# A causal softmax convolution and a gated two-matrix product on one core: an earlier pace for block 5's input, paired tiles in the narrow round, one evicting engine per pair in block 0, and another order of the first copies

## Chip, core and metric

The kernel runs on one core of a Trainium2 chip. The metric is the device time of one execution in microseconds (us), as the median of several executions; lower is better. A profile is taken from one separate execution, so its times belong to that execution.

## What is computed

The input `x` is 8 sequences of 3904 rows and 192 columns. Each group of 24 columns (a head, 8 of them) has 7 taps; the taps pass through a softmax, and every output row is the weighted sum of the row and the six before it. The result, flattened to 31232 rows, goes through a gated product and two more matrices.

```
w   = softmax(weight, axis=-1)                      # 8 heads x 7 taps
c[b, s, h, :] = sum_k w[h, k] * x_pad[b, s + k, h, :]   # six zero rows before each sequence
a, b = c @ w1, c @ w2                               # 192 -> 1024
h    = (a * b) @ w3                                 # 1024 -> 1024
out  = h @ w_out                                    # 1024 -> 192
```

Inputs and output are fp32; the kernel multiplies in bf16 and accumulates in fp32.

## The kernel before

The kernel is one program whose instruction order on every engine is written out by hand. `w3 @ w_out` is folded into one 1024x192 matrix `W_sb` once (`w3_product`, from a transposed `w3T`), so that the main work per row is one product with `w1`, one with `w2`, an elementwise product, and one with `W_sb`.

**Rows.** The 31232 rows are cut into two streams of 15616 rows (`NS = 2`), which lie in the two halves of the partitions. A round `R` is 512 columns (rows of the input) of both streams; there are 31 rounds, the last of them, round 30, has 256 columns. Rounds go in groups of four.

**Convolution.** It works on windows of 64 rows of which 58 are new, in blocks of windows (`SIZES`: 6, 4, 8, 10, 8, then six of 36, then 20). `load_x(b)` fetches a block's windows with DMAs from the POOL queue into `xb` tiles (five buffers). `conv` multiplies them with band matrices `Aband`, made from the taps by `band`, into PSUM, and ScalarE (ACT) or VectorE (DVE) copies the result to `convo`. In blocks 0 to 4 TensorE transposes `convo` into `xT` (`pe_transpose`, `joint_transposes`). From block 5 on, `store` writes `convo` to a DRAM tensor `rows` and `transposes` reads it back transposed by DMA from SP's queue.

**PSUM.** It is used as four pairs of banks (`banks()` takes a pair, `drained` gives it back). `move_all(p, moves, fs)` copies the parts of one pair with the engines named in `fs`, in order; `V`, `A` and `P` are copies on DVE, ACT and GpSimd (POOL).

**First product.** `first_part` makes one tile of 128 of the 1024 columns: for each of `w1` and `w2` six matmuls, three slices of 64 input columns (`k`) times two streams, 12 in all; ACT copies the first factor to `asb` (L390), DVE multiplies it with the second factor from PSUM into `abT` (L391). `first_rest` does the same for several tiles side by side in one pair of banks; before, only the rest of round 0 uses it. **Second product:** `second_product` multiplies `abT` by `W_sb` (L445), ACT evicts it (L450), a DMA writes it out.

**Prologue.** Block 0 is convolved, evicted, transposed and multiplied as early as its data arrive. `w1` and `w2` come in four parts of 256 columns. The first is cast from an fp32 tile; the other three are fetched by POOL's queue into partitions 0 to 63 (`load_w`) and copied to partitions 64 to 127 by POOL (`copy_w`, L193). The order on POOL is the order of these lines (L195 to L202):

```
    load_w(1)
    cast_w(1, 1, nc.gpsimd.tensor_copy)
    load_w(2)
    load_x(2, between=[seq((copy_w, 1, i, nc.gpsimd.tensor_copy) for i in range(2))])
    load_w(3)
    ...
```

`between` places the two copies of part 1 between the two DMAs of block 2. After that POOL issues `load_x(3)`, the two halves of `w3` to the DRAM tensor `w3rows` (L470), `load_x(4)` and more. SP's queue holds 16 DMA transposes of `w3rows` into `w3T` (L474): eight 128-column tiles of the first half of its rows, then eight of the second half. Each half of them waits for its half of `w3rows`.

**Pace.** At L568 POOL copies two elements of `w3T` to a tiny tile `pace` just ahead of `load_x(5)` and `load_x(6)`, so that these ten DMAs start only when a certain transpose of `w3T` has landed:

```
    P(out=pace, in_=w3T[0:1, JT - 3, DFF - 2:DFF])
    load_x(5)
    load_x(6)
    first_product(3)
    ...
    zero(5)
    for jt in range(JT):
        w3_product(jt)
```

`JT` is 8, and the columns read belong to the second half, so this is the fourteenth transpose. `zero(5)` clears six rows in one of block 5's tiles, once per stream, behind all of `load_x(5)` and `load_x(6)` on POOL (L575). `w3_product(jt)` for `jt` below 4 reads transposes 1 to 8 and from `jt = 4` on transposes 9 to 16. The second products of rounds 0 to 3 follow, with the convolution of block 5 between them, three heads at a time.

**End.** The last group is rounds 28 to 30; its first products run in the order 30, 28, 29, and its second products close the program.

Of the kernel before, what the change touches and what calls it, by code (L numbers as in the profile page):

```python
# [16 lines left out]
def kernel(  # L17
# [10 lines left out]
    nc = tc.nc  # L28
# [42 lines left out]
    def banks():  # L71
        p = free.pop(0)
        return p, pairs[:, NS * p:NS * p + NS, :]
# [4 lines left out]
    def drained(p):  # L78
        assert p not in free
        free.append(p)  # L80
# [7 lines left out]
    def seq(fs):  # L88
        def run():
            for f, *a in fs:  # L90
                f(*a)
        return run
# [12 lines left out]
    def load_x(b, parts=(0, 1), between=()):  # L105
        between = list(between)
        tiles = xb_of.setdefault(b, [])
        zeros_of = zero_rows.setdefault(b, [])
        for i0, n in [v for e, v in enumerate(halves_of(b)) if e in parts]:
            xb = work.tile([128, n, D], BF16, tag="xb", bufs=5, name="xb")  # L110
            w = 0
            while w < n:
                i = i0 + w
                m = min(n - w, WB - i % WB)
                at_end = i + m == NWIN
                if at_end:
                    m -= 1
                if m:
                    for r in range(NS):
                        nc.gpsimd.dma_start(out=xb[Q * r:Q * r + Q, w:w + m, :],  # L120
                                            in_=x_spans(r, i, m))
                        if between:
                            between.pop(0)()
                if i % WB == 0:
                    zeros_of += [(xb, 0, w), (xb, 1, w)]
                w += m
                if at_end:
                    nc.gpsimd.memset(xb[Q:128, w, :], 0.0)
                    t = tok(NWIN - 1) - PAD
                    nc.gpsimd.dma_start(out=xb[0:Q, w, :], in_=x_rows[t:t + Q, :])  # L130
                    nc.gpsimd.dma_start(out=xb[Q:Q + PAD + LAST, w, :],
                                        in_=x_rows[TS + t:TS + t + PAD + LAST, :])
                    w += 1
            if len(halves_of(b)) == 1:
                tiles += [(xb, 0), (xb, SIZES[b] // 2)]
            else:
                tiles.append((xb, 0))
# [233 lines left out]
    def width(R):  # L371
        return min(CH, TS - R * CH)

    def first_part(R, ft, c0, c1, ks=tuple(range(NP))):
        ab = abT_of[R]
        r0 = (R * CH) % RING
        pq = []
        for i in range(2):
            q, p = banks()
            pq.append((q, p))  # L380
            for k in ks:
                for r in range(NS):
                    rs = slice(Q * r, Q * r + Q)
                    nc.tensor.matmul(  # L384
                        p[:, r, c0:c1], wd[i][rs, k, ft * 128:(ft + 1) * 128],
                        xT[k][rs, r0 + c0:r0 + c1],
                        start=(k == ks[0]), stop=(k == ks[-1]))
        (qa, pa), (qb, pb) = pq
        asb = work.tile([128, NS, CH], BF16, tag="asb", bufs=3, name="asb")
        nc.scalar.copy(out=asb[:, :, c0:c1], in_=pa[:, :, c0:c1])  # L390
        nc.vector.tensor_tensor(out=ab[:, ft, :, c0:c1], in0=asb[:, :, c0:c1],  # L391
                                in1=pb[:, :, c0:c1], op=ALU.mult)
        drained(qa)
        drained(qb)

    def first_rest(R, fts, c0, c1):
        ab = abT_of[R]
        r0 = (R * CH) % RING
        n, ne = c1 - c0, len(fts)
        assert ne * n <= CH  # L400
        pq = []
        for i in range(2):
            q, p = banks()
            pq.append((q, p))
            for e, ft in enumerate(fts):
                for k in range(NP):
                    for r in range(NS):
                        rs = slice(Q * r, Q * r + Q)
                        nc.tensor.matmul(  # L409
                            p[:, r, e * n:e * n + n], wd[i][rs, k, ft * 128:(ft + 1) * 128],  # L410
                            xT[k][rs, r0 + c0:r0 + c1], start=(k == 0), stop=(k == NP - 1))
        (qa, pa), (qb, pb) = pq
        asb = work.tile([128, NS, CH], BF16, tag="asb", bufs=3, name="asb")
        nc.scalar.copy(out=asb[:, :, 0:ne * n], in_=pa[:, :, 0:ne * n])
        a, b = (t[:, :, 0:ne * n].rearrange("p r (e c) -> p r e c", e=ne) for t in (asb, pb))
        nc.vector.tensor_tensor(
            out=ab[:, fts[0]:fts[0] + ne, :, c0:c1].rearrange("p e r c -> p r e c"),
            in0=a, in1=b, op=ALU.mult)
        drained(qa)
        drained(qb)  # L420

    def first_tile(R):
        abT_of[R] = work.tile([128, JT, NS, CH], BF16, tag="abT", bufs=GROUP, name="abT")
# [80 lines left out]
    def move_all(p, moves, fs):  # L504
        for f, m in zip(fs, moves):
            move(f, m)
        drained(p)

    def joint_transposes(b):
        n = SIZES[b] // 2  # L510
        assert n * NP <= 2 * CH // 64
        convo = convo_of[b]
        p, tps = banks()
        tps = bf16(tps)
        t0, moves = tok(FIRST[b]), []
        for k in range(NP):
            for w in range(n):
                nc.tensor.transpose(
                    out=tps[:, k * n + w, :],
                    in_=convo[:, w, k].rearrange("p r g -> p (r g)"), identity=ident)  # L520
            src = tps[:, k * n:k * n + n, :].rearrange("p w (c s) -> p c w s", c=2)
# [12 lines left out]
    first_part(0, 0, 0, EARLY, (0, 2, 1))  # L534
    move_all(*joint_transposes(1), (A, A, V))
    first_part(0, 1, 0, EARLY)
    first_rest(0, range(2), EARLY, CH)
    load_w3(0)
    for i in range(2):
        copy_w(3, i, P)  # L540
# [27 lines left out]
    P(out=pace, in_=w3T[0:1, JT - 3, DFF - 2:DFF])  # L568
    load_x(5)
    load_x(6)  # L570
    first_product(3)
# [70 lines left out]
```

## Time and profile before

| what | value |
|---|---|
| median of three runs | 523.0 us (522.9 to 523.83) |
| the profiled execution, its own time | 523.71 us |
| its span (first to last instruction) | 522.0 us |
| TensorE busy | 514.2 us, 98% of the span |
| VectorE busy | 358.1 us |
| ScalarE busy | 326.1 us |
| GpSimd busy | 58.6 us |
| granted TensorE clock | 0.998 |

The span leaves 1.7 us of the execution's own time outside. PE is TensorE and PEld its weight loads, DVE VectorE, ACT ScalarE, POOL GpSimd, SP SyncE; a name with a q (SPq, POOLq) is that engine's queue of DMA issues. L489 is line 489 of the kernel before. In the chain of waits each row is a start, a duration and what ran; in the timeline a row is start, duration, engine, line, operation, output and input, the count, and in brackets how long the engine had been idle and what ended that.

### The profile page before, as it was taken

To read this page: it belongs to the slowest core of one execution; us is meant where nothing else is said; L and a number is where in the kernel's file an instruction comes from. 1 tells how busy PE (TensorE), PEld (TensorE's weight loads), DVE (VectorE), ACT (ScalarE), POOL (GpSimd) and SP (SyncE) were. 2 spreads that over 40 slices of the span, in tenths; PEclk is the share of its full clock that TensorE was granted. 3 is DMA by queue.
4 is the path that set the end of the run, shared out by engine and by line. 5 is a ranking of instruction groups with operands and counts; after the bars stand their busy time and mean duration, and the time that the engine had idled before them with its cause. 6 is when DMAs were issued, how large, how long until landed. Compare 5 with 4: busy or idle time off the path is not lost.

```text
span 522.0 us, 13021 instructions
## 1 busy us (share of the span) xinstructions
PE 514.2 (98%) x5576; PEld 340.5 (65%) x5576; DVE 358.1 (69%) x347; ACT 326.1 (62%) x414; POOL 58.6 (11%) x98
## 2 busy tenths in 40 slices
PE   7999999999999999999999999999999999999997
PEld 4555788444894558845588455884558845599567
DVE  6778646799538995389953899438993299912870
ACT  6887642777437774377743777337774377735762
POOL 8601622030000200003000020001200000000000
PEclk9999999999999999999999999999999999999999
DMA  8979998699556973569645698456824532034004
GB/s 115 157 145 125 148 225 219 161 209 147 129 156 164 111 99 102 152 165 124 86 110 148 158 126 84 118 146 156 102 45 122 153 96 31 17 104 140 1 3 151
DMA packets 133420, 64.61 MB, mean 124 GB/s; under 512 B 90304, under 2 KB 132642, under 8 KB 133298
## 3 DMA queue, kind: packets, MB, share of 16 engines
q1 hardware_dynamic: 94320, 44.06, 35.0%
q0 software_dynamic: 38896, 19.62, 28.8%
q8 instruction: 43, 0.70, 0.6%
q14 instruction: 15, 0.12, 0.1%
q10 hardware_dynamic: 146, 0.10, 0.1%
HBM read 33.25 MB, written 36.52 MB: 134 GB/s over the span
## 4 chain that ended last, share of the span: by engine, by line
PE 90%; issue 3%; DMA 2%; DVE 2%; ACT 1%; POOL 1%; ACTq 0%; POOLq 0%; DVEq 0%
PE pairs L384 56%; PE pairs L445 31%; PE pairs L291 3%; DMA xb<-in_x_dram 2%; DVE abT L391 1%; ACT asb L390 1%; PE pairs L207 1%; POOL xb L120 0%; DVE cprod L248 0%; PE pairs L344 0%; ACT convo L312 0%; DVE convo L489 0%; POOL rows L335 0%; POOL wo_b L567 0%; PE pairs L409 0%
## 5 line engine op out<-in xcount | busy, mean ns | idle before, releaser
L391 DVE TENSOR_TENSOR abT<-asb,pairs 128x1024 bf16<-128x1024 bf16 (+2 forms) x248 | 297.9, 1201 | 76.8 <-ACT asb L390 39.9
L384 PE MATMUL pairs<-xT,wd 64*128 64x512 bf16 (+2 forms) x2976 | 319.4, 372 | 0.8 <-DVE abT L391 0.3
L390 ACT CAST asb<-pairs 128x1024 bf16<-128x1024 f32 (+2 forms) x248 | 247.1, 996 | 67.4 <-PE pairs L384 66.7
L384 PEld LDWEIGHTS <-wd 64*128 64x128 bf16 x2976 | 162.2, 94 | 151.4 <-issue 2.3
L445 PE MATMUL pairs<-W_sb,abT 128*128 128x192 bf16 x1952 | 166.1, 246 | 0.0
L445 PEld LDWEIGHTS <-abT 128*128 128x128 bf16 x1952 | 159.6, 98 | 9.7 <-issue 9.7
L450 ACT COPY osb<-pairs 128x384 f32<-128x384 f32 x122 | 58.3, 478 | 116.0 <-PE pairs L445 116.0
L312 DVE CAST convo<-pairs 128x864 bf16<-128x864 f32 (+5 forms) x67 | 50.8, 815 | 68.5 <-PE pairs L291 64.3
L120 POOL DMA_DIRECT2D xb<-in_x_dram x42 | 32.2, 782 | 6.4 <-PE pairs L384 3.7
L597 POOL COPY pace<-abT 1x2 bf16<-1x2 bf16 x10 | 1.8, 176 | 239.6 <-DVE abT L391 239.6
L291 PE MATMUL pairs<-xb,Aband 64*64 64x432 bf16 (+5 forms) x384 | 17.7, 284 | 0.5 <-POOL xb L575 0.5
L291 PEld LDWEIGHTS <-Aband 64*64 64x64 bf16 x384 | 7.2, 106 | 7.8 <-issue 6.6
L312 ACT CAST convo<-pairs 128x512 bf16<-128x512 f32 (+4 forms) x15 | 8.1, 584 | 1.3 <-PE pairs L291 1.2
L457 POOL DMA_DIRECT2D out_dram<-osb x8 | 6.1, 759 | 18.4 <-ACT osb L450 18.0
L450 DVE COPY osb<-pairs 128x192 f32<-128x192 f32 x1 | 0.4, 357 | 11.1 <-PE pairs L445 11.1
L480 PEld LDWEIGHTS <-w3T 128*128 128x128 bf16 x64 | 5.2, 98 | 0.4 <-issue 0.4
L480 PE MATMUL pairs<-wo_b,w3T 128*128 128x192 bf16 x64 | 5.5, 246 | 0.0
L344 PE MATMUL pairs<-ident,convo 128*128 128x128 bf16 x48 | 3.9, 219 | 1.4 <-DVE convo L489 1.3
L344 PEld LDWEIGHTS <-convo 128*128 128x128 bf16 x48 | 2.9, 97 | 3.2 <-DVE convo L489 1.6
L193 POOL COPY wd<-wd 64x768 bf16<-64x768 bf16 x6 | 4.8, 840 | 0.9 <-DMA wd<-in_moe_w_dram 0.9
L207 PE MATMUL pairs<-zeros 128*128 128x512 bf16 x8 | 3.8, 628 | 1.1 <-DVE ones L155 1.1
L482 ACT CAST W_sb<-pairs 128x192 bf16<-128x192 f32 x8 | 2.6, 319 | 2.8 <-PE pairs L480 2.8
(56 smaller groups left out, 42.0 us busy)
## 6 DMA issues: line engine op xcount, KB each, us to landing
out_dram<-osb SPq DMA_DIRECT2D x52, 384.0 KB
xb<-in_x_dram POOLq DMA_DIRECT2D x18, 432.0 KB, 7.5
rows<-convo SPq DMA_DIRECT2D x8, 648.0 KB
out_dram<-osb POOLq DMA_DIRECT2D x8, 384.0 KB, 4.8
w3rows<-in_moe_w_dram POOLq DMA_DIRECT2D x2, 1024.0 KB, 11.7
xb<-in_x_dram POOLq DMA_DIRECT2D x6, 240.0 KB, 5.3
rows<-convo SPq DMA_DIRECT2D x4, 324.0 KB
xT<-rows SPq DMA_TRANSPOSE x81
```

Source lines behind the costliest of these rows:

```text
L120: nc.gpsimd.dma_start(out=xb[Q * r:Q * r + Q, w:w + m, :], in_=x_spans(r, i, m))
L207: nc.tensor.matmul(t[:, j % 2, :], zeros, zeros[:, 0:1].to_broadcast([128, CH]), start=True, stop=True)
L291: nc.tensor.matmul(view(slice(Q * c, Q * c + Q), r)[:, :, j * G:(j + 1) * G], band_of(h, r), xb[Q * r:Q * r + Q, w0:w0 + n, h * G:(h + 1) ...
L312: f[e % len(f)](out=dst, in_=part)
L344: nc.tensor.transpose(out=tps[:, w, :], in_=convo[:, w, k].rearrange("p r g -> p (r g)"), identity=ident)
L384: nc.tensor.matmul(p[:, r, c0:c1], wd[i][rs, k, ft * 128:(ft + 1) * 128], xT[k][rs, r0 + c0:r0 + c1], start=(k == ks[0]), stop=(k == ks[-1]))
L390: nc.scalar.copy(out=asb[:, :, c0:c1], in_=pa[:, :, c0:c1])
L391: nc.vector.tensor_tensor(out=ab[:, ft, :, c0:c1], in0=asb[:, :, c0:c1], in1=pb[:, :, c0:c1], op=ALU.mult)
L445: nc.tensor.matmul(ops[:, (g - g0) * D:(g - g0) * D + D], ab[:, jt, r, g * 128:(g + 1) * 128], W_sb[:, jt, :], start=(jt == 0), stop=(jt = ...
L450: f(out=osb[:, g0:g0 + per, :].rearrange("p g d -> p (g d)"), in_=ops[:, 0:per * D])
L457: queue.dma_start(out=out[t0:t0 + ng * 128, :].rearrange("(g p) d -> p g d", p=128), in_=osb)
L480: nc.tensor.matmul(wps[:, 0, 0:D], w3T[:, gt, jt * 128:(jt + 1) * 128], wo_b[:, gt, :], start=(gt == 0), stop=(gt == JT - 1))
```

## The change

Five edits.

- POOL issues both DMAs of block 2 and then makes the two copies of part 1 (`between` goes away).
- In block 0, the pair of the first four heads is evicted by DVE alone and the pair of the last four by ACT alone; before, each pair was shared by both. The three transposed tiles are evicted in the order 0, 1, 2 by DVE, DVE, ACT, and the first tile of the product takes its slices in that order.
- `joint_transposes` (block 1) puts the third slice, which DVE evicts, into the pair's second bank.
- `first_part` and `first_rest` become one function over a list of tiles. `first_product` takes `512 // width` tiles at a time, so round 30 makes four pairs of 128-column tiles in place of eight single ones; other rounds are as before.
- `pace` reads the fourth transpose of the second half, the twelfth, in place of the fourteenth.

```diff
-    load_x(2, between=[seq((copy_w, 1, i, nc.gpsimd.tensor_copy) for i in range(2))])
+    load_x(2)
+    for i in range(2):
+        copy_w(1, i, nc.gpsimd.tensor_copy)
     load_w(3)
...
-    def first_part(R, ft, c0, c1, ks=tuple(range(NP))):
...
+    def first_factor(R, i, fts, c0, c1):
+        n, r0 = c1 - c0, (R * CH) % RING
+        assert len(fts) * n <= CH
+        q, p = banks()
+        for e, ft in enumerate(fts):
+            for k in range(NP):
                 for r in range(NS):
                     rs = slice(Q * r, Q * r + Q)
                     nc.tensor.matmul(
-                        p[:, r, c0:c1], wd[i][rs, k, ft * 128:(ft + 1) * 128],
-                        xT[k][rs, r0 + c0:r0 + c1],
-                        start=(k == ks[0]), stop=(k == ks[-1]))
+                        p[:, r, e * n:e * n + n], wd[i][rs, k, ft * 128:(ft + 1) * 128],
+                        xT[k][rs, r0 + c0:r0 + c1], start=(k == 0), stop=(k == NP - 1))
+        return q, p[:, :, 0:len(fts) * n]
...
+    def first_part(R, fts, c0, c1):
+        a, b = (first_factor(R, i, fts, c0, c1) for i in range(2))
+        first_times(R, fts, c0, c1, first_cast(*a), *b)
...
-        for ft in fts:
-            first_part(R, ft, 0, width(R))
+        N = width(R)
+        step = CH // N
+        for ft in fts[::step]:
+            first_part(R, list(range(ft, ft + step)), 0, N)
...
+        B2 = CH // 64
+        at = [0, n, B2]
...
-                    out=tps[:, k * n + w, :],
+                    out=tps[:, at[k] + w, :],
...
-    move_all(*conv(0, 0, 4, ()), (V, A))
-    move_all(*conv(0, 4, 4, ()), (A, V))
-    for k, f in ((0, A), (2, V), (1, V)):
+    move_all(*conv(0, 0, 4, ()), (V, V))
+    move_all(*conv(0, 4, 4, ()), (A, A))
+    for k, f in enumerate((V, V, A)):
         p, *m = pe_transpose(0, k)
...
-    first_part(0, 0, 0, EARLY, (0, 2, 1))
+    first_part(0, [0], 0, EARLY)
...
-    P(out=pace, in_=w3T[0:1, JT - 3, DFF - 2:DFF])
+    P(out=pace, in_=w3T[0:1, JT // 2 - 1, DFF - 2:DFF])
```

`first_cast` is ACT's copy to `asb` and `first_times` DVE's product, as they were inside `first_part` and `first_rest`.

More of the change, by code (lines that the diff above doesn't have):

```diff
@@ L103, in x_spans, with load_x @@
                        ap=[[D, Q], [ST * D, m], [1, D]])
-    def load_x(b, parts=(0, 1), between=()):
-        between = list(between)
+    def load_x(b, parts=(0, 1)):
         tiles = xb_of.setdefault(b, [])
@@ L121, in load_x @@
                                             in_=x_spans(r, i, m))
-                        if between:
-                            between.pop(0)()
                 if i % WB == 0:
@@ L372, in width @@
         return min(CH, TS - R * CH)
-    def first_part(R, ft, c0, c1, ks=tuple(range(NP))):
[L375 to L381, printed above, removed]
+    def first_factor(R, i, fts, c0, c1):
[4 more added lines that the diff above has]
+            for k in range(NP):
                 for r in range(NS):
@@ L384, in first_part, with first_cast @@
                     nc.tensor.matmul(
[L385 to L388 removed]
+                        p[:, r, e * n:e * n + n], wd[i][rs, k, ft * 128:(ft + 1) * 128],
+                        xT[k][rs, r0 + c0:r0 + c1], start=(k == 0), stop=(k == NP - 1))
+        return q, p[:, :, 0:len(fts) * n]
+    def first_cast(qa, pa):
@@ L389, in first_part @@
         asb = work.tile([128, NS, CH], BF16, tag="asb", bufs=3, name="asb")
-        nc.scalar.copy(out=asb[:, :, c0:c1], in_=pa[:, :, c0:c1])
-        nc.vector.tensor_tensor(out=ab[:, ft, :, c0:c1], in0=asb[:, :, c0:c1],
-                                in1=pb[:, :, c0:c1], op=ALU.mult)
+        asb = asb[:, :, 0:pa.shape[2]]
+        nc.scalar.copy(out=asb, in_=pa)
         drained(qa)
-        drained(qb)
[L396 to L420, printed above, removed]
@@ new lines, in first_cast, with first_times @@
+        return asb
+    def first_times(R, fts, c0, c1, asb, qb, pb):
+        ab, ne = abT_of[R], len(fts)
+        if ne == 1:
+            dst = ab[:, fts[0], :, c0:c1]
+        else:
+            dst = ab[:, fts[0]:fts[0] + ne, :, c0:c1].rearrange("p e r c -> p r e c")
+            asb, pb = (t.rearrange("p r (e c) -> p r e c", e=ne) for t in (asb, pb))
+        nc.vector.tensor_tensor(out=dst, in0=asb, in1=pb, op=ALU.mult)
+        drained(qb)
+    def first_part(R, fts, c0, c1):
+        a, b = (first_factor(R, i, fts, c0, c1) for i in range(2))
+        first_times(R, fts, c0, c1, first_cast(*a), *b)
@@ L510, in joint_transposes @@
         n = SIZES[b] // 2
-        assert n * NP <= 2 * CH // 64
+        B2 = CH // 64
+        at = [0, n, B2]
+        assert 2 * n <= B2
         convo = convo_of[b]
@@ L518, in joint_transposes @@
                 nc.tensor.transpose(
-                    out=tps[:, k * n + w, :],
+                    out=tps[:, at[k] + w, :],
                     in_=convo[:, w, k].rearrange("p r g -> p (r g)"), identity=ident)
-            src = tps[:, k * n:k * n + n, :].rearrange("p w (c s) -> p c w s", c=2)
+            src = tps[:, at[k]:at[k] + n, :].rearrange("p w (c s) -> p c w s", c=2)
             moves.append((xT[k][:, t0:t0 + 2 * n * ST].rearrange("p (c w s) -> p c w s", c=2, w=n),
@@ L533 @@
     first_tile(0)
-    first_part(0, 0, 0, EARLY, (0, 2, 1))
+    first_part(0, [0], 0, EARLY)
     move_all(*joint_transposes(1), (A, A, V))
-    first_part(0, 1, 0, EARLY)
-    first_rest(0, range(2), EARLY, CH)
+    first_part(0, [1], 0, EARLY)
+    first_part(0, [0, 1], EARLY, CH)
     load_w3(0)
```

## Prediction

> **What bounds the kernel now.** I read the page first, then the chain of waits, then the timeline where the chain leaves TensorE, last the DMA queues in windows. The page gives the frame.
>
> ```profile
> span 522.0 us, 13021 instructions
> PE 514.2 (98%) x5576; PEld 340.5 (65%) x5576; DVE 358.1 (69%) x347; ACT 326.1 (62%) x414; POOL 58.6 (11%) x98
> ```
>
> TensorE is busy for nearly all of the span, so an edit gains only where TensorE waits and nothing else holds the next step. The chain of waits (start, duration, what ran) shows those places.
>
> ```profile
> 7.43 0.57 DVE convo L489
> ...
> 8.03 0.55 ACT convo L489 x2
> ...
> 8.60 0.57 DVE convo L489
> ...
> 9.21 0.51 PE pairs L344 x6
> 9.72 0.37 PE pairs L291 x32
> 10.09 0.99 PE pairs L384 x12
> ...
> 13.46 1.96 PE pairs L384 x18
> ...
> 57.62 10.35 DMA xb<-in_x_dram
> ...
> 91.64 41.55 PE pairs L384 x384
> ...
> 478.41 1.11 PE pairs L384 x18
> 479.52 0.68 DVE abT L391
> ...
> 505.04 13.32 PE pairs L445 x160
> ```
>
> Three places: copies of block 0 one after another (7.43 to 9.17), the DMA of block 5's input (57.62 to 67.97), and DVE in the narrow round (478.41 to 505.04). Between the second and the third the chain is TensorE without a hole, so time won before 68 us stays won if block 5's input comes as much earlier.
>
> **Block 0's copies and the copy order.** The timeline of this stretch:
>
> ```profile
> 6.21 1.69 ACT L189 CAST wd<-wfirst 64x768 bf16<-64x768 f32 x2
> 8.45 0.47 ACT L489 COPY xT<-pairs 128x348 bf16<-128x348 bf16 x1
> 8.60 0.56 DVE L489 CAST convo<-pairs 128x384 bf16<-128x384 f32 x1 [0.61 <-ACT convo L489]
> 10.14 0.48 ACT L489 CAST convo<-pairs 128x384 bf16<-128x384 f32 x1 [1.22 <-PE pairs L291]
> 10.68 0.74 ACT L390 CAST asb<-pairs 128x696 bf16<-128x696 f32 x1
> 10.77 1.59 POOL L193 COPY wd<-wd 64x768 bf16<-64x768 bf16 x2 [0.86 <-DMA wd<-in_moe_w_dram]
> 11.45 0.88 DVE L391 TENSOR_TENSOR abT<-asb,pairs 128x696 bf16<-128x696 bf16 x1 [0.71 <-ACT asb L390]
> 12.31 0.68 POOL L120 DMA_DIRECT2D xb<-in_x_dram  x1
> ```
>
> Within a pair the engines take turns: ACT starts at 8.03 when DVE's copy of the first pair ends at 8.00, and DVE starts on the second pair at 8.60 when ACT ends at 8.57. With one engine per pair the two pairs go side by side. DVE ends its large copy at 8.00 as before; its small one (192 elements) costs between half of 0.57 and all of it; I take 0.3, so 8.3. ACT is free at 6.21 + 1.69 = 7.90; its small copy takes 0.55 / 2 = 0.27, the large one 0.48 (the row at 10.14, same shape), so it ends at about 8.67. The last transposes start at 8.7, not 9.21. Three of them (some 0.3) and block 1's convolution (0.37) end at 9.4. ACT evicts the last transposed slice in 0.47, by 9.5; the first product has then done two slices and ends its other 8 of 12 matmuls (0.66) at about 10.3, where it ended at 11.08 before: 0.8 earlier. ACT, though, has block 1's copy (0.48) behind that slice and starts `asb` at about 10.05, not 10.68: 0.63 earlier, and DVE and the next tiles hang on that. I take **0.6**, with 0.3 below (DVE's wait of 0.61 less ACT's small copy of 0.27) and 0.8 above.
>
> The bank for block 1's third slice I count at nothing: DVE copies it behind its own product, 11.45 to 12.33, so ACT has not been what it waits for. The three slices' order is in the sum above. POOL: the second DMA of block 2 (0.68 to issue) moves into the 0.86 that POOL idles before the copies, so the copies stay at 10.77 to 12.36 and everything issued behind them on POOL, the next part of the weights, block 3 and `w3`, goes out about 0.6 earlier. Tile 2, the first to need those copies, starts at 13.46 - 0.6 = 12.86; its cover is 0.5. As `w3` is fetched 0.6 earlier, its transposes start 0.6 earlier too; were that lost, the next part would come out smaller by it.
>
> **The pace.** The stretch around block 5, SP's queue, POOL and PE:
>
> ```profile
> 48.48 1.26 SPq L474 DMA_TRANSPOSE w3T<-w3rows  x1
> ...
> 51.09 1.26 SPq L474 DMA_TRANSPOSE w3T<-w3rows  x1
> ...
> 53.70 1.26 SPq L474 DMA_TRANSPOSE w3T<-w3rows  x1
> 53.86 0.18 POOL L568 COPY pace<-w3T 1x2 bf16<-1x2 bf16 x1 [12.02 <-DMA w3T<-w3rows]
> 54.39 6.21 POOL L120 DMA_DIRECT2D xb<-in_x_dram  x8 [0.36 <-issue]
> 59.56 5.45 PE L480 MATMUL pairs<-wo_b,w3T 128*128 128x192 bf16 x64
> 67.58 0.37 PE L291 MATMUL pairs<-xb,Aband 64*64 64x432 bf16 x2
> 68.52 0.25 POOL L575 MEMSET xb<- 6x192 bf16 x1 [0.26 <-DMA xb<-in_x_dram]
> 68.83 0.70 PE L291 MATMUL pairs<-xb,Aband 64*64 64x432 bf16 x9 [0.17 <-POOL xb L575]
> 72.20 0.74 PE L291 MATMUL pairs<-xb,Aband 64*64 64x432 bf16 x12
> ```
>
> Block 5's first 12 matmuls begin at 67.58 and end at 69.53, 1.95 where the next 12 (72.20) take 0.74: TensorE waits **1.21** for the input and the memset behind it. The twelfth transpose is issued 51.09 - 48.48 = 2.61 before the fourteenth, so `pace` and the first DMA come 2.61 earlier, on top of the 0.6. But at that time transposes still run, and they share the 16 DMA engines:
>
> ```profile
> q1 hardware_dynamic: 8704, 2.10, 45.4%
> ...
> q1 hardware_dynamic: 1094, 0.26, 31.7%
> ...
> q0 software_dynamic: 1486, 0.56, 157.9%
> ...
> q0 software_dynamic: 764, 0.29, 97.6%
> q1 hardware_dynamic: 501, 0.13, 41.6%
> ...
> q0 software_dynamic: 1220, 0.46, 156.6%
> q1 hardware_dynamic: 33, 0.00, 1.8%
> ```
>
> These are packets, MB and share of the engines' time in windows: the transposes from 27 to 57 us; of these, 53.3 to 57; then input DMAs (q0) alone, 173 to 176; input beside a transpose, 182.5 to 185; and input from 107.5 to 110 with a transpose issued. Input packets lag their issue by about 1.6 (issue at 54.39, first packets near 56), so in the present frame they would start at 53.3, with 1094 of 8704 packets, two of the 16 transposes, still to go. Alone, input moves 1486 / 3 = 495 packets per us; beside 501 transpose packets it moved 764 in 2.5 us where 1238 were due: 0.95 lost per transpose packet, so 1094 cost 1094 x 0.95 / 495 = 2.1. While the input's stream ramps up the loss is smaller; I take **1.85**, with 1.0 below and 2.6 (the whole lead) above. The input then lands 0.6 + 2.61 - 1.85 = 1.36 earlier. TensorE arrives 0.6 earlier and had 1.21 to wait, so at most 1.81 can be gained here; 1.36 is below that, and 0.45 of the wait remains. **Gain up to 69.5 us: 1.36**, from 0.3 (loss 2.6, transposes 0.3 earlier) to 1.8.
>
> The Trainium skill speaks against expecting more: DMA: Bandwidth & Descriptors, section "Queues, rings and completion order", has each DMA engine take turns between its queues packet by packet. By that rule each transpose packet would cost one input packet, 2.2 in all, and the gain here would be 1.0. The trace agrees at 182.5 (764 to 501) and not at 107.5 (1220 to 33).
>
> The last transpose: it feeds `w3_product` from the fifth column tile on, at 59.56 + 5.45 x 4.9 / 8 = 62.9, or 62.3 with the 0.6. Issued at 53.70, it lands by the lag of the fourteenth (51.09 to 53.86) near 56.4, or 55.8 with the 0.6. It would be late only if delayed by over 6; sharing as at 182.5 delays it by some 3, the 2.5 us of blocking at 107.5 on top gives 5.5. So the cover is thin, and I count nothing but keep it as the slower rival. Nothing else waits for POOL's earlier `pace`.
>
> **The narrow round.** From 478.41 to 505.04 are 26.63. At the pace of a full group, 41.55 / 384 = 0.1082 per matmul of 512 columns, its 192 full and 96 half-width matmuls take 20.78 + 5.19 = 25.97. DVE is the brake: 0.68 per half tile against 12 x 0.0541 = 0.65 on TensorE. In pairs round 30 has the instructions of half a full round, where no wait shows. I take **0.66**. Nothing is the lower end: 12 matmuls of 348 columns took 0.99 where the rate gives 0.88, and half-width ones may have such an excess of 12%. Loss is excluded: no engine gets more to do.
>
> **Sum.** 1.36 + 0.66 = 2.02. The profiled execution's span goes from 522.0 to 520.0, its own time from 523.71 to 521.7. It lies 0.7 above the median of 523.0; I put the same 2.0 off the median: **521.0**. With each term's ends: 0.3 + 0 to 1.8 + 0.66, thus 520.5 to 522.7.
>
> **Rivals.** (1) *The last transposes are blocked for as long as input is queued.* Blocks 5 and 6 are 36 windows each, 64 rows x 2 streams x 36 x 192 columns x 2 bytes = 1.77 MB, and at 0.56 MB in 3 us both take 19 us, from 52.7 to 71.7. TensorE would stand in `w3_product` from 62.3 to about 72.5, 10 late; it no longer waits for input, and 0.66 is won at the end: 10.2 - 1.8 - 0.66, about 7.7 slower, 530.7. For it speaks 107.5 to 110 with 33 packets to 1220; against it, at 182.5 the transpose went through with most of the input still ahead. It decides once the last transpose lands after 62.3; a delay of 9 takes the whole gain away. (2) *The early start only trades places*: the DMA engines do the same work before block 5 is in, the loss is the full 2.6 or over, and only 0.0 to 0.6 is won there: 521.7 to 522.5, say 522.0. For it: the loss by rule is already 2.2. Against: the transposes alone use the engines for a third to a half. (3) *The early copies reach nothing*, because some input of blocks 1 to 4 is late and the input of block 5 with it: 1.0 less, 522.1.
>
> **Chances.** Forecast 0.62, rival 1 0.18, rival 2 0.16, rival 3 0.04. About 0.2%, or 1.05 us, is what a measurement of this kernel can tell. The forecast lies over that; of rivals 2 and 3 I give 0.06 to faster and 0.14 to no change: faster 0.68, same 0.14, slower 0.18. The range: 520.3 at the low end, 0.2 beyond the full gain for the spread between executions, to 522.9, which takes in rivals 2 and 3 and the smallest gain; rival 1 is left out.
>
> **What would show it.** In the changed profile `asb` of the first tile starts near 10.05; `pace` ends its wait near 50.7; transposes 15 and 16 show issue times above 1.26; block 5's first 12 matmuls take about 1.2 and end near 68.2; round 30 shows no DVE on the chain and 25.97 up to the last second products. Wrong would be a hole in `w3_product` between its fourth and fifth tile (rival 1), or block 5's end at 69 or later (rival 2).

## The result and the profile after

The changed kernel takes **521.65 us** (median of 6 executions, 521.1 to 522.14); the kernel before took 523.5 on the same occasion (6 executions, 522.9 to 524.05). The ratio is 0.9965, 95% interval 0.9952 to 0.9978: 1.8 us faster. The profiled execution took 522.07 and had this page:

```profile
span 520.4 us, 13006 instructions
PE 513.5 (99%) x5576; PEld 339.8 (65%) x5576; DVE 357.5 (69%) x343; ACT 325.7 (63%) x410; POOL 58.4 (11%) x98
```

The span is 1.6 shorter, and the matmuls are the same 5576: what went is waiting. The chain of waits of the changed kernel (start, duration, what ran) says where. Its lines are numbered anew: L290 is the convolution, L381 the first product, L467 `w3_product`, L432 the second product.

```profile
5.19 4.20 DMA xb<-in_x_dram
...
9.43 0.44 PE pairs L290 x31
9.87 0.99 PE pairs L381 x12
...
59.41 5.39 PE pairs L467 x64
...
67.75 0.70 PE pairs L290 x9
...
90.57 41.55 PE pairs L381 x384
...
477.34 26.07 PE pairs L381 x288
503.41 13.32 PE pairs L432 x160
```

Block 0's copies, block 5's input and DVE in round 30 have left the chain. In front stands a new row, block 1's input, which lands at 9.39. The round's 288 matmuls take 26.07 where they took 26.63 from 478.41 to 505.04: **0.56**. The row 90.57 stood at 91.64: **1.07** came before it. Together 1.63, the span's 1.6.

The timeline of the prologue after (L476 is a copy out of PSUM, L389 makes `asb`, L457 issues a half of `w3`):

```profile
7.52 0.82 DVE L476 CAST convo<-pairs 128x384 bf16<-128x384 f32 x2 [0.25 <-PE pairs L290]
7.79 0.68 ACT L476 CAST convo<-pairs 128x192 bf16<-128x192 f32 x2
9.43 0.44 PE L290 MATMUL pairs<-xb,Aband 64*64 64x48 bf16 x31 [0.31 <-DMA xb<-in_x_dram]
10.46 0.74 ACT L389 CAST asb<-pairs 128x696 bf16<-128x696 f32 x1
16.29 0.55 POOL L457 DMA_DIRECT2D w3rows<-in_moe_w_dram  x1
```

The two pairs of block 0 are now evicted side by side, and both are out at 8.47 where the second ended at 9.16. In this execution TensorE then stands 0.31 for block 1's input, and `asb` starts only 0.22 earlier than before (10.68). The timeline around block 5 (L461 is a transpose of `w3`, L557 the `pace` copy, L564 the memset of `zero(5)`):

```profile
46.34 2.45 SPq L461 DMA_TRANSPOSE w3T<-w3rows  x1
51.22 0.17 POOL L557 COPY pace<-w3T 1x2 bf16<-1x2 bf16 x1 [9.60 <-DMA w3T<-w3rows]
51.75 7.17 POOL L119 DMA_DIRECT2D xb<-in_x_dram  x9 [0.36 <-PE pairs L381]
52.74 1.26 SPq L461 DMA_TRANSPOSE w3T<-w3rows  x1
59.34 5.45 PE L467 MATMUL pairs<-wo_b,w3T 128*128 128x192 bf16 x64
67.37 1.09 PE L290 MATMUL pairs<-xb,Aband 64*64 64x432 bf16 x12
67.45 0.25 POOL L564 MEMSET xb<- 6x192 bf16 x1 [0.34 <-DMA xb<-in_x_dram]
```

The twelfth transpose is issued at 46.34 and `pace` is released at 51.22, 4.88 later; the last is issued at 52.74 (53.70 in the kernel before). `w3_product` runs through in 5.45. Block 5's first 12 matmuls end at 68.46 instead of 69.53, and 1.09 - 0.74 = 0.35 of waiting is left. What the DMA queues moved meanwhile (packets, MB, share of the engines' time; q0 is the input, q1 the transposes), in the windows 54 to 55, 55 to 56, 56 to 57 and 58 to 59 us:

```profile
q0 software_dynamic: 248, 0.10, 87.0%
q1 hardware_dynamic: 12, 0.00, 1.6%
...
q0 software_dynamic: 476, 0.18, 156.2%
q1 hardware_dynamic: 19, 0.00, 2.6%
...
q0 software_dynamic: 500, 0.19, 156.8%
q1 hardware_dynamic: 6, 0.00, 1.1%
...
q0 software_dynamic: 277, 0.11, 85.5%
q1 hardware_dynamic: 271, 0.07, 53.4%
```

For 3 us what is left of the transposes, about the last one, hardly moves; in the last of these windows both queues get about as many packets. The Trainium skill, DMA: Bandwidth & Descriptors, section "Queues, rings and completion order", has an engine take turns between its queues packet by packet. If the profile's packets are the ones meant there, which no run here shows, 277 to 271 agrees with that and 500 to 6 does not.

### The profile page after: what moved, and what is told of

Its sections match the earlier page's. It is cut to its first block, busy times and chain, and to the rows that moved or that the text cites. A ratio compares the mean times of both kernels' runs of the same rounds, so it can differ in the third digit from the quotient of the medians.

```text
span 520.4 us, 13006 instructions
## 1 busy us (share of the span) xinstructions
PE 513.5 (99%) x5576; PEld 339.8 (65%) x5576; DVE 357.5 (69%) x343; ACT 325.7 (63%) x410; POOL 58.4 (11%) x98
## 4 chain that ended last, share of the span: by engine, by line
PE 95%; ACT 1%; DVE 1%; DMA 1%; POOL 1%; issue 0%; POOLq 0%; ACTq 0%
PE pairs L381 59%; PE pairs L432 32%; PE pairs L290 3%; DVE abT L400 1%; PE pairs L467 1%; ACT asb L389 1%; DMA xb<-in_x_dram 1%; PE pairs L343 0%; POOL xb L172 0%; POOL xb L182 0%; ACT convo L311 0%; POOL xb L119 0%; ACT xT L355 0%; POOL diag L176 0%; PE pairs L507 0%
## 5 line engine op out<-in xcount | busy, mean ns | idle before, releaser
L400 DVE TENSOR_TENSOR abT<-asb,pairs 128x1024 bf16<-128x1024 bf16 (+1 forms) x245 | 298.1, 1217 | 76.8 <-ACT asb L389 60.5
L381 PE MATMUL pairs<-xT,wd 64*128 64x512 bf16 (+3 forms) x3000 | 319.7, 371 | 0.7 <-DVE abT L400 0.3
L389 ACT CAST asb<-pairs 128x1024 bf16<-128x1024 f32 (+1 forms) x245 | 247.1, 1009 | 67.7 <-PE pairs L381 67.3
L381 PEld LDWEIGHTS <-wd 64*128 64x128 bf16 x3000 | 162.3, 94 | 151.8 <-issue 1.8
L432 PE MATMUL pairs<-W_sb,abT 128*128 128x192 bf16 x1952 | 166.1, 246 | 0.0
L432 PEld LDWEIGHTS <-abT 128*128 128x128 bf16 x1952 | 159.6, 98 | 9.7 <-issue 9.7
L290 PE MATMUL pairs<-xb,Aband 64*64 64x432 bf16 (+5 forms) x384 | 17.5, 284 | 0.4 <-DMA xb<-in_x_dram 0.3
L290 PEld LDWEIGHTS <-Aband 64*64 64x64 bf16 x384 | 7.2, 106 | 7.5 <-issue 6.3
L467 PEld LDWEIGHTS <-w3T 128*128 128x128 bf16 x64 | 5.2, 98 | 0.4 <-issue 0.4
L467 PE MATMUL pairs<-wo_b,w3T 128*128 128x192 bf16 x64 | 5.5, 246 | 0.0
```

The costliest lines, as they stand in the source:

```text
L290: nc.tensor.matmul(view(slice(Q * c, Q * c + Q), r)[:, :, j * G:(j + 1) * G], band_of(h, r), xb[Q * r:Q * r + Q, w0:w0 + n, h * G:(h + 1) ...
L381: nc.tensor.matmul(p[:, r, e * n:e * n + n], wd[i][rs, k, ft * 128:(ft + 1) * 128], xT[k][rs, r0 + c0:r0 + c1], start=(k == 0), stop=(k == ...
L389: nc.scalar.copy(out=asb, in_=pa)
L400: nc.vector.tensor_tensor(out=dst, in0=asb, in1=pb, op=ALU.mult)
L432: nc.tensor.matmul(ops[:, (g - g0) * D:(g - g0) * D + D], ab[:, jt, r, g * 128:(g + 1) * 128], W_sb[:, jt, :], start=(jt == 0), stop=(jt = ...
L467: nc.tensor.matmul(wps[:, 0, 0:D], w3T[:, gt, jt * 128:(jt + 1) * 128], wo_b[:, gt, :], start=(gt == 0), stop=(gt == JT - 1))
```

## The experiments

All of them ran on one chip, apart from the result above, on four occasions with the kernel before beside them (92 executions of it, medians 523.93 to 524.08). A column of the table gives the executions whose mean granted TensorE clock was 0.997 or less, because that turned out to matter. The last three columns are of one profiled execution each: `w3_product`'s start, the end of POOL's second memset behind block 5's input (start plus 0.25), and the end of block 5's first 12 matmuls.

| kernel | median us | ratio to before (95%) | low clock | `w3_product` | memset ends | 12 end |
|---|---|---|---|---|---|---|
| before (profile: the one ahead of the prediction) | 524.0 | 1 | 54 of 92 | 59.56 | 68.77 | 69.53 |
| changed (the result above) | 521.65 | 0.9965 (0.9952 to 0.9978) | 0 of 6 | 59.34 | 67.70 | 68.46 |
| after_again: changed | 521.99 | 0.9968 (0.9956 to 0.998) | 2 of 12 | 60.14 | 66.10 | 68.90 |
| pace_only | 523.98 | 1.0002 (0.9993 to 1.0012) | 8 of 11 | 59.52 | 68.85 | 69.60 |
| pairs_only | 523.52 | 0.999 (0.9979 to 1.0001) | 8 of 12 | 59.59 | 67.56 | 68.36 |
| front_only | 522.6 | 0.9981 (0.997 to 0.9993) | 2 of 12 | 60.74 | 66.22 | 69.50 |
| pool_only | 523.97 | 0.9995 (0.998 to 1.001) | 9 of 12 | 61.13 | 68.80 | 69.90 |
| evict_only | 523.14 | 0.9988 (0.9976 to 1.0001) | 0 of 12 | 58.89 | 67.47 | 68.22 |
| warm_before | 523.4 | 0.999 (0.9979 to 1.0002) | 0 of 11 | 59.83 | 68.73 | 69.48 |
| conv1_late | 523.32 | 0.9999 (0.9988 to 1.0011) | 5 of 12 | 60.82 | 67.49 | 69.59 |
| pace14 | 521.67 | 0.9959 (0.9943 to 0.9974) | 1 of 8 | 58.95 | 66.62 | 67.71 |
| wo_early | 521.26 | 0.9954 (0.9936 to 0.9972) | 0 of 6 | 58.88 | 65.66 | 67.64 |
| wo_warm | 521.44 | 0.9949 (0.9931 to 0.9967) | 0 of 6 | 59.03 | 65.40 | 67.80 |
| wo_warm14 | 521.29 | 0.9946 (0.993 to 0.9963) | 0 of 6 | 58.83 | 65.71 | 67.59 |

**pace_only** is the kernel before with the twelfth transpose for `pace`.

```diff
-    P(out=pace, in_=w3T[0:1, JT - 3, DFF - 2:DFF])
+    P(out=pace, in_=w3T[0:1, JT // 2 - 1, DFF - 2:DFF])
```

> The kernel before with the pace on the twelfth transpose and nothing else. Theory (the pace carries the gain at block 5): pace ends its wait near 51.2, block 5's memsets start near 67.0 and 67.5 (68.0 and 68.5 before), block 5's first 12 matmuls end near 68.5 (69.5 before), span 521.0. Rival (the lead is lost to the transposes that still run, and the earlier fetch of w3 carries the gain): memsets within 0.3 of before, span 521.8 to 522.0.

Measured 1.0002: no gain. In its timeline:

```profile
68.60 0.25 POOL L575 MEMSET xb<- 6x192 bf16 x1 [0.27 <-DMA xb<-in_x_dram]
68.90 0.70 PE L291 MATMUL pairs<-xb,Aband 64*64 64x432 bf16 x9 [0.18 <-POOL xb L575]
```

The matmuls start at 68.90, those of the kernel before at 68.83. `pace` was released at 52.02, and the memset came 16.58 later where the kernel before has 14.66 (53.86 to 68.52): 1.9 is lost while the last transposes are still under way, and what is left of the lead doesn't show.

**front_only** is the changed kernel with the fourteenth transpose and single tiles in round 30: evictions and POOL's order alone.

```diff
-        step = CH // N
-        for ft in fts[::step]:
-            first_part(R, list(range(ft, ft + step)), 0, N)
+        for ft in fts:
+            first_part(R, [ft], 0, N)
...
-    P(out=pace, in_=w3T[0:1, JT // 2 - 1, DFF - 2:DFF])
+    P(out=pace, in_=w3T[0:1, JT - 3, DFF - 2:DFF])
```

> The changed kernel with the pace back on the fourteenth transpose and the narrow round in single tiles: only block 0's copies, the bank of block 1's third slice and the order on POOL. Theory: TensorE arrives at block 5 about 0.2 earlier, which is lost in its wait; the input lands by as much earlier as the transposes run earlier. If they keep the 0.7 by which the first of them is earlier, block 5 ends 0.7 earlier and the span is 521.3; if the transposes lose it again to the fetch of w_out that runs among them, block 5 ends 0.0 to 0.2 earlier and the span is 521.8 to 522.0. I lean to the second.

Measured 0.9981, 1.0 us, the largest share of any part. Its profiled execution showed something else. The windows 9 to 10, 10 to 11, 11 to 12 and 12 to 13 us (length, then busy share of PE, PEld, DVE, ACT and POOL; the column after them is the granted clock):

```profile
9.00:10.00 1.00, 0.69 (x34) 0.55 (x32) 0.31 (x1) 0.45 (x1) 1.00 (x3) 0.68 1.10 126
10.00:11.00 1.00, 1.00 (x22) 0.52 (x14) 0.56 (x1) 0.48 (x1) 1.00 (x2) 0.50 1.03 130
11.00:12.00 1.00, 1.00 (x9) 0.30 (x6) 0.00 (x0) 0.74 (x1) 1.00 (x2) 0.50 0.98 100
12.00:13.00 1.00, 1.00 (x12) 0.73 (x12) 0.86 (x2) 0.39 (x2) 1.00 (x3) 0.62 1.11 127
```

Of the full clock 0.32, 0.50, 0.50 and 0.38 are missing, 1.70 us in all: TensorE ran at half its clock for 3.4 us, `w3_product` came at 60.74, and the input, in at 66.22, was not awaited. That is a second cause of lost time, which the profile of the kernel before doesn't show and the counts of executions do.

**pairs_only** is the kernel before with round 30 in pairs of tiles.

```diff
-        for ft in fts:
-            first_part(R, ft, 0, width(R))
+        step = CH // width(R)
+        for ft in fts[::step]:
+            if step > 1:
+                first_rest(R, range(ft, ft + step), 0, width(R))
+            else:
+                first_part(R, ft, 0, width(R))
```

> The kernel before with round 30 in pairs of tiles and nothing else. Theory: the stretch from the round's first matmul to the last second products takes 26.07 in place of 26.63, the span is 521.4, and all before the round is as before. Rival (the pairs only move the wait to the change of rounds): 26.4 or more.

Measured 0.999, 0.5 us, with an interval that just reaches 1; on its chain the round takes 26.07 (477.24 to 503.31), the 0.56 of the changed kernel. The same profile has a surprise at block 5, with a prologue that is that of the kernel before:

```profile
67.31 0.25 POOL L579 MEMSET xb<- 6x192 bf16 x1 [0.28 <-DMA xb<-in_x_dram]
67.62 0.74 PE L291 MATMUL pairs<-xb,Aband 64*64 64x432 bf16 x12
```

The memset comes 1.21 earlier than in the kernel before (68.52), and TensorE doesn't wait at all. So block 5's input lands over 1 us earlier or later from one execution to another.

**conv1_late** is the changed kernel with block 1's convolution and its eviction behind the first tile; it was to show what waiting for block 1's input costs.

```diff
-    move_all(*conv(1, 0, H, "streams"), (A, V))
     first_tile(0)
     first_part(0, [0], 0, EARLY)
+    move_all(*conv(1, 0, H, "streams"), (A, V))
```

> The changed kernel with block 1's convolution moved behind the first tile's product on TensorE. Theory (the copies of block 0 did win their 0.6, and it was lost to the landing of block 1's input, for which TensorE stood 0.3 with the product queued behind): the first tile's asb starts at 10.05 or earlier (10.46 in the changed kernel), TensorE reaches w3_product 0.1 to 0.4 earlier than the changed kernel. Rival (the landing costs nothing, the copies were mis-sized): asb at 10.4 or later.

```profile
9.80 0.74 ACT L389 CAST asb<-pairs 128x696 bf16<-128x696 f32 x1 [0.41 <-PE pairs L381]
10.63 0.48 ACT L476 CAST convo<-pairs 128x384 bf16<-128x384 f32 x1
11.37 0.55 DVE L476 CAST convo<-pairs 128x384 bf16<-128x384 f32 x1
```

`asb` starts 0.66 earlier than in the changed kernel's profile, but block 1's copies now queue behind `asb` and its product, and the second tile of work is late: `w3_product` at 60.82, 0.9999. The place was a bad one, and what the wait for block 1 costs is not settled by this run.

**pace14** is the changed kernel with the fourteenth transpose again (the second half of front_only's diff); **after_again** is the changed kernel once more, on the same occasion.

> The changed kernel with the pace back on the fourteenth transpose, nothing else undone. Theory (the earlier pace gains 0 to 0.4, since the input's stream from pace to memset takes 16.2 to 16.6 with it and 14.4 to 14.7 without): 0 to 0.4 us slower than the changed kernel, the span of executions at full clock 519.5 to 520.8, pace to second memset 14.7 or less. Rival (what the prediction had, a gain of 0.76 by the pace): 0.7 or more slower.

> The changed kernel as it is, beside the other variants on one chip. Theory (two things vary from one execution to the next: whether TensorE's granted clock falls to half for some 3 us in the prologue, at 1.2 us, and when block 5's input lands; the change makes both rarer): at most 3 of 12 executions show a clock of 0.997 or less, where the kernel before shows over half of its own; ratio 0.995 to 0.997. Rival (the gain is the same in every execution): both kernels spread alike and are 1.6 to 1.8 us apart at every clock.

pace14 measured 521.67 and 0.9959, after_again 521.99 and 0.9968: without the earlier pace the kernel is as fast or faster.

```profile
10.07 0.74 ACT L389 CAST asb<-pairs 128x696 bf16<-128x696 f32 x1
58.95 5.45 PE L467 MATMUL pairs<-wo_b,w3T 128*128 128x192 bf16 x64
66.37 0.25 POOL L564 MEMSET xb<- 6x192 bf16 x1 [0.26 <-DMA xb<-in_x_dram]
66.97 0.74 PE L290 MATMUL pairs<-xb,Aband 64*64 64x432 bf16 x12
```

Here block 1's input was in time: `asb` at 10.07 and `w3_product` 0.61 earlier than before. The input is ready 0.35 before TensorE comes, with the late pace, and block 5's matmuls end at 67.71, 1.82 earlier than in the kernel before.

**wo_early** is the changed kernel with the fetch of `w_out` (`wo_b`) issued behind the second half of `w3`, not just ahead of `pace`.

```diff
+    nc.gpsimd.dma_start(out=wo_b, in_=wor)
...
-    nc.gpsimd.dma_start(out=wo_b, in_=wor)
     P(out=pace, in_=w3T[0:1, JT // 2 - 1, DFF - 2:DFF])
```

> The changed kernel with the fetch of w_out issued on POOL right behind the second half of w3, ahead of the wait for block 4's copies, so that it no longer runs among the transposes. Theory (the fetch of w_out blocks the transposes for 2 to 3 us and makes the twelfth land 4.9 behind its issue, not 2.7): the twelfth transpose lands 2.7 to 3 behind its issue, pace ends its wait 1 to 2 us earlier than 51.2, block 5's second memset starts before 66.8, no wait of TensorE for block 5, 0.3 us faster than the changed kernel. Rival (the first transposes are held up by as much): pace ends its wait at 51 or later, no gain.

```profile
47.70 0.17 POOL L557 COPY pace<-w3T 1x2 bf16<-1x2 bf16 x1 [7.45 <-DMA w3T<-w3rows]
66.90 0.74 PE L290 MATMUL pairs<-xb,Aband 64*64 64x432 bf16 x12
```

The twelfth transpose (issued 44.09) now lands 3.6 behind its issue, not 4.88. In the four profiles with the twelfth transpose and the fetch at its old place the lag is 4.84 to 7.03, in the two with the early fetch 3.56 and 3.61, so the fetch of `w_out` accounts for part of it. `pace` is released 3.5 earlier than in the changed kernel, and block 5's matmuls start 0.07 earlier than in pace14: again nothing for the input to win. The median of 521.26 lies 0.4 from pace14's, within both intervals.

**warm_before** is the kernel before with three matmuls on zeros (`warm`) behind the first transpose of block 0, where TensorE stands idle for block 0's copies.

```diff
+        if k == 0:
+            warm(3)
```

> The kernel before with three more matmuls on zeros behind the first transposes of block 0, where TensorE waits 0.8 us for the copies; they cost nothing else and feed nothing. Theory (the idle stretch near 9 us lets the granted clock fall to half): at most 3 of 12 executions at a clock of 0.997 or less against over half for the kernel before, median 0.5 us faster or more unless the input of block 5 takes its place. Rival (the clock falls for another reason): as many executions at the lower clock as before, no gain.

The windows 7 to 8, 8 to 9 and 9 to 10 us of the kernel before, and 8 to 9 of this one:

```profile
7.00:8.00 1.00, 0.59 (x32) 0.40 (x31) 0.84 (x2) 0.87 (x2) 0.96 (x3) 1.00 1.44 169
8.00:9.00 1.00, 0.34 (x3) 0.17 (x3) 0.40 (x1) 0.89 (x3) 1.00 (x2) 1.00 1.01 120
9.00:10.00 1.00, 0.79 (x38) 0.67 (x38) 0.56 (x3) 0.00 (x0) 0.91 (x2) 1.00 0.76 93
```

```profile
8.00:9.00 1.00, 0.99 (x6) 0.38 (x6) 0.45 (x1) 0.88 (x3) 1.00 (x2) 1.00 0.97 119
```

None of 11 executions had a low clock, against 54 of 92. So the idle stretch brings the fall about. But the median gained only 0.5 (0.999, the interval reaches 1.0002): in its profile the nine matmuls behind the memset start at 68.78, waiting for it. The wait for block 5's input took the place of the clock. `w3_product` comes 0.27 later than in the kernel before (59.83); that is not the filler, since TensorE runs 0.04 ahead until 31 us (on its chain a row of the first product starts at 31.00, in the kernel before at 31.04).

**pool_only** is the kernel before with POOL's new order alone (both DMAs of block 2, then the two copies).

> The kernel before with the new order on POOL (both DMAs of block 2, then the two copies) and nothing else. Theory (this order alone makes the transposes of w3 run earlier and takes TensorE's wait for block 5 away; it does nothing to the granted clock): the sixteenth transpose is issued at 52.5 or earlier (52.45 to 53.70 in four kernels with the old order), no wait of more than 0.4 at block 5, as many executions at a clock of 0.997 or less as the kernel before, executions at full clock 522.4 to 523.0. Rival (the evictions make the transposes earlier): sixteenth at 53.3 or later, the wait of up to 1.2 remains, executions at full clock up to 524.3.

```profile
11.32 1.59 POOL L193 COPY wd<-wd 64x768 bf16<-64x768 bf16 x2 [0.75 <-DMA wd<-in_moe_w_dram]
```

Measured 0.9995 (0.998 to 1.001): alone, nothing that can be told. The copies waited 0.75 for their part of the weights, which in this execution landed 0.55 later than in the kernel before (10.77); the order gives nothing when that DMA is the last to come. The clock was low in 9 of 12, in the profiled one too, where `w3_product` came at 61.13 and the input was not awaited. The last transpose was issued at 52.54, between what the theory (52.5 or earlier) and the rival (53.3 or later) expected. The three executions at full clock took 522.55 to 522.64, as the theory had it.

**evict_only** is the kernel before with the evictions of block 0, the slices' order and block 1's third slice as changed, and the rest as before.

```diff
-    move_all(*conv(0, 0, 4, ()), (V, A))
-    move_all(*conv(0, 4, 4, ()), (A, V))
-    for k, f in ((0, A), (2, V), (1, V)):
+    move_all(*conv(0, 0, 4, ()), (V, V))
+    move_all(*conv(0, 4, 4, ()), (A, A))
+    for k, f in enumerate((V, V, A)):
```

> The kernel before with block 0's evictions, the order of the slices and the bank of block 1's third slice as changed; the order on POOL, the fourteenth transpose for pace and single tiles in the narrow round as before. Theory (the end of block 5's convolution is set by the later of TensorE's arrival and the landing of block 5's input; the evictions move only the first, the order on POOL only the second): the first tile's asb starts at 9.9 to 10.5, not 10.68; at most 3 of 10 executions show a granted clock of 0.997 or less; the w3 rows are still issued near 17.2, the last transpose near 53.0 to 53.7, so block 5's second memset stays at 68.0 to 68.6 and TensorE waits there, 0.5 to 1.8. The median is 522.3 to 523.4, ratio 0.998 to 0.9995, all of it from executions without a fall of the clock. Rival (the order on POOL does nothing, the evictions bring all that the front part of the change brings): no wait at block 5 beyond 0.2, w3_product near 59.0, block 5's first 12 matmuls end by 68.3, ratio 0.9975 or less.

```profile
10.00 0.74 ACT L390 CAST asb<-pairs 128x696 bf16<-128x696 f32 x1
67.22 0.25 POOL L564 MEMSET xb<- 6x192 bf16 x1 [0.27 <-DMA xb<-in_x_dram]
67.52 0.70 PE L291 MATMUL pairs<-xb,Aband 64*64 64x432 bf16 x9 [0.18 <-POOL xb L564]
```

Measured 0.9988, 0.6 us, and no low clock in 12 executions. `asb` starts at 10.00 and `w3_product` at 58.89; at block 5 TensorE still waits, 0.57 (the 12 matmuls run from 66.91 to 68.22, 1.31 for 0.74), in one of the fastest executions (522.41). The others reach 525.02 at full clock. The rival, 0.9975 or less without a wait, is out. The memset came 0.8 earlier than the theory had it: the first half of `w3` went out at 16.71 here and at 17.20 in the kernel before, with the same order on POOL; the last transpose was issued at 52.70, where 53.0 to 53.7 was expected.

**wo_warm** and **wo_warm14** are wo_early with two matmuls on zeros (`warm(2)`) ahead of block 0's transposes, the second with the fourteenth transpose for `pace`.

```diff
+    warm(2)
...
+    nc.gpsimd.dma_start(out=wo_b, in_=wor)
...
-    nc.gpsimd.dma_start(out=wo_b, in_=wor)
-    P(out=pace, in_=w3T[0:1, JT // 2 - 1, DFF - 2:DFF])
+    P(out=pace, in_=w3T[0:1, JT - 3, DFF - 2:DFF])
```

> The changed kernel with the fetch of w_out ahead of the transposes and two more matmuls on zeros in front of block 0's transposes, where TensorE waits 0.5 us for DVE; they feed nothing. Theory (both of the things that vary are then out of the way): no execution at a clock of 0.997 or less, no wait for block 5, median 521.0 to 521.3, 0.3 to 0.8 us under the changed kernel's 521.99. Rival (the two matmuls push the transposes back, or the clock falls all the same): 521.6 or more.

> As the one before, with the pace on the fourteenth transpose. Theory (with the transposes unhindered the input is in time with either pace, and the earlier pace is worth nothing): the same median within 0.3 us, pace to second memset 14.0 to 14.8. Rival (the earlier pace is needed): 0.5 us slower or more, a wait at block 5.

They measured 521.44 (521.25 to 521.77) and 521.29 (521.14 to 521.59): the narrowest spreads of all, and for the third time the pace makes no difference. wo_warm's median lies between what its theory (521.3 at most) and its rival (521.6 at least) expected. wo_warm14 has the lowest ratio, 0.9946 (0.993 to 0.9963), 2.8 us below the kernel before. Against the changed kernel's 0.9968 the intervals overlap, and the two weren't run on one occasion, so that it beats the changed kernel is likely and not settled.

## Why the prediction was right, and where it wasn't

The forecast was 521.0 and faster; measured were 521.65 and 521.99, inside the range, by the ratios 1.8 and 1.7 us faster where 2.0 was predicted. The sum was near, in part by luck. Of its three terms one shows no gain when it is tested, and falls of the granted clock, of which the prediction knew nothing, decide over part of the median. Even the pair of profiles hides this: it has 1.07 won up to 69.5 us where 1.36 was predicted, but pace14 wins more there without the pace.

- **Block 0's copies: right.** `asb` was predicted at 10.05, `w3_product` 0.6 earlier. Where block 1's input is in time, it is 10.07 and 10.00, and 0.61 and 0.67 earlier (pace14, evict_only). In the changed kernel's own profile it was 10.46 and 0.22, because block 1's input landed at 9.39 and became the bound: the prediction had no term for that.
- **POOL's order: not settled.** Alone it gives 0.9995 with an interval on both sides of 1. The last transpose is issued at 50.67 to 52.74 in the six profiles with the new order and at 52.45 to 53.70 in the five with the old one (`w_out` fetched at its old place in all of them). That speaks for the order, but the ranges overlap and the evictions changed along with it in five of the six.
- **The pace: wrong.** The term was 1.36 to 69.5 us, 0.76 of it beyond the early start. Three steps did not hold. The lead of 2.61 took the fourteenth transpose's lag of 2.77 (51.09 to 53.86) for the twelfth's, which was 4.88; so `pace` came at 51.22, not 50.7. The loss to the transposes, 1.85 predicted, is no fixed amount: from `pace` to the second memset it is 14.66 in the kernel before, 16.23 here and 16.58 in pace_only (1.6 and 1.9 lost, two transposes still to be issued), 17.71 and 17.54 in wo_early and wo_warm, but 14.80 and 14.87 in after_again and conv1_late, where one or none was left to issue when `pace` came. And the wait of 1.21 that was to be won was that of one execution. With the earlier prologue and the old pace the input is in time (pace14: ready at 66.62, wanted at 66.97). Three comparisons of twelfth and fourteenth, pace_only, after_again against pace14, wo_warm against wo_warm14, differ by -0.05, +0.3 and +0.15 us: no gain, where 0.76 was predicted. For the pace alone rival 2 held, that the early start only trades places: pace_only's second memset starts at 68.60, that of the kernel before at 68.52.
- **The last transposes: the cover held.** What was left of them was blocked for 3 us and shared the engines after that, as the prediction had put it at worst, but `w3_product` shows no hole: rival 1 is out. Their issue times, 1.26, do not show it; the packet counts do.
- **The narrow round: right**, 0.56 for 0.66. The excess of half-width matmuls over the rate, which was its lower end, is the rest.
- **What was missing: the granted clock.** The kernel before has its clock fall in the prologue in 54 of 92 executions, most of them 523.8 to 524.3. At full clock 26 of 38 lie at 522.43 to 523.46 and 12 at 523.64 to 524.55; their median is 523.04, that of all 92 is 524.03. Nine of the 54 show 0.993 and take 525.04 to 525.53; 3.4 us at half the clock cost 0.0033 of the mean, so these have room for two falls.

Both things that vary meet in one rule: block 5's convolution starts at the later of TensorE's arrival, which a fall of the clock delays, and its input's landing, which varies by over 1 us. The table bears it out. In all 14 profiled executions the end of the 12 matmuls is the later of `w3_product`'s start plus 8.76 and the memset's end plus 0.75, to within 0.02. The memset is the later one in before, changed, pace_only, evict_only and warm_before, TensorE's arrival in the other nine. What follows is nearly fixed: an execution's own time less that end is 454.18 to 454.21 in the six with single tiles in round 30 and 453.60 to 453.64 in seven of the eight with pairs. The eighth, after_again, has 453.94 and one more wait on its chain, for transposed rows until 102.02. So what differs between these executions is decided before 70 us, but for the 0.57 of the narrow round.

That explains why a cure of only one side gains so little: warm_before (no fall, the input awaited), pool_only and pace_only (meant to bring the input earlier; in their profiles it is in at 68.80 and 68.85, in that of the kernel before at 68.77, and the clock is low in 9 of 12 and 8 of 11), evict_only (no fall, the input awaited, executions from 522.35 to 525.02). The changed kernel has the fall in 2 of 18. The parts alone, 0.6, 0.3, 0.5 and -0.1, sum to 1.3 of the 1.7 to 1.8; the rest is what such a rule would give, but the intervals would allow a plain sum too.

What stays open: why the fall comes in some executions and not in others, what POOL's order gives, and what block 1's late input costs.

## What to carry to other kernels

A wait that one profiled execution shows at a DMA may be one draw from a spread as large as the wait; look at the spread of the plain times before putting its whole length into a sum. Where two causes meet in one "the later of the two", test the parts one by one and together, since each alone can measure as nothing. And an idle stretch in a prologue can cost more than its length when it lets the clock fall: filling it (no fall in 11 executions here) or shortening it (none in 12) shows first in the spread of the times.

## What the runs showed of the hardware that was not expected

The granted clock went to 0.50 though TensorE had no long gap. In the profiles of front_only, after_again and pool_only the fall begins at 9.35, 8.24 and 10.22 us and lasts 3.41 us each time. In the 3.41 us ahead of it TensorE is busy for 2.40, 2.31 and 2.15, and its longest gap is 0.61, 0.61 and 0.82. The Trainium skill, TensorE: Matmul & The Clock Gate, section "Part 1: The HAM clock gate", has the half clock follow at least one idle window of about 3.4 us that runs freely against the kernel. The half clock agrees (0.50), and the fall has that length. A fall that begins at a different place each time, or not at all, fits a free-running window. An idle window does not fit, since over 2 of the 3.41 us ahead of each fall hold work; how little work is too little these runs do not show. Three matmuls on zeros, in the microsecond that TensorE of the kernel before is busy for 0.34, were enough to end it: no low clock in 11 executions.

DMA transposes that are queued beside input from POOL's queue were held up almost completely for 3 us in the changed kernel's profile (37 packets to 1224 from 54 to 57 us, when about one transpose was left) and for 2 us in pace_only's (33 to 814 from 55 to 57); after that the changed kernel has a near even share (271 to 277 from 58 to 59).
